# Second products split over two loops, and one more block of attention in row form

## The chip, the cores and the metric

The kernel runs on one core of one Trainium2 chip. The metric is the device time of one execution in microseconds; the median of three runs of the kernel before is 274.97 us (273.76 to 275.08). The profile is of one further execution, with its own time. Engines are named as in the profile: PE is TensorE (PEld its weight loads), DVE VectorE, ACT ScalarE, POOL GpSimd and SP SyncE; the last two mostly issue DMAs here.

## The reference: linear attention, then a two-layer network

Inputs are q, k, v of shape 8 x 8 x 576 x 64 (batch, head, position, width) and a norm weight g of 64; w_in is 512 x 2048, w_out 2048 x 512, alpha 2048, all in float32.

```
kv  = einsum('bhsd,bhse->bhde', k, v)
o   = einsum('bhsd,bhde->bhse', q, kv)
o   = o / sqrt(mean(o*o, axis=-1) + 1e-6) * g_norm
x   = o.transpose(0, 2, 1, 3).reshape(4608, 512)
h   = x @ w_in
g   = maximum(h, 0) + alpha * minimum(h, 0)
out = g @ w_out
```

There is no softmax. The network takes most of the arithmetic: two products of 4608 x 512 x 2048.

## The kernel before

The 4608 rows of x are cut into nine windows of 512 (W), numbered w = 0 to 8; the eight batches are called blocks b and have 576 rows, so a window covers the end of one block and the start of the next. Everything on TensorE is float16 with float32 sums in PSUM.

**First product.** For a window, a loop of 16 units u makes h in groups of 128 of the 2048 columns: four matmuls of 512 columns into one PSUM bank (`m1_mm`, L507). `m1_evac` then has ScalarE write max(-h, 0) (L514) and VectorE add it, weighted by 1 - alpha, to h; that gives `gt`, the activation in float16 (L518). From w=2 on, two banks, h1 and h2, take turns for h (three in w=1). For windows from W_ROW on, the first unit is "late": the first 384 columns (`m1_cols`, L530), some second products, then the last 128 columns.

**Second product.** Window 0 uses plain matmuls (`y_mm`, L539). Windows 1 to 8 use a Winograd form of Strassen's method on 2 x 2 blocks: seven products instead of eight, each of 16 matmuls of 256 columns (`prod_mm`, L688). Products 1 and 2 read `gt` and `w_out` alone. Products 6, 7, 5 and 3 read sums of `gt` blocks that VectorE makes (`s_sum`, s1 to s4, L623 to L629). Results collect in three sets called X (products 1, 2), Y (6, 7, 4) and Z (5, 3); `y_read` takes them out of PSUM: p1 and c11 on ScalarE, u2, u3, c21, c22 and c12 on VectorE. c11 to c22 are the output's quarters, which are then stored. In the kernel before, all seven products of window w-1 are made in the loop of window w, seven matmuls to each unit, and those of window 8 after the last loop. X and Z share one bank and Y has the other (`ps_y` and h0, swapped from window to window).

**Attention.** Attention of window w+1 is worked into the loop of w by tables from the unit to the step (`ATT_1`, `ROW_AT`, `QT_AT`). Windows 0 to 2 take the "column" form: q is transposed on TensorE (`step_t`, L327), k·v is made by head pairs (`step_kv`, L371) and masked on VectorE, q·kv comes out transposed (`step_ot`, L393), squares are made on ScalarE (L400) and summed by a matmul with a mask (`ssq_mm`, L416), and `norm` (L429) multiplies by 1/rms and g into xt. From W_ROW = 3 on comes the "row" form: q is transposed by DMAs on SP (`dma_t`, L361), `row_kv` (L1001) makes k·v by heads, `rows_mm` (L452) makes four tiles of 128 rows, `rows_sq` squares a tile on ScalarE (L463), `rows_ssq` sums it by head on VectorE (L469), `rows_rs` makes 1/rms on ScalarE (L479), and `rows_norm` multiplies on VectorE (L487) and issues a transposing DMA on SP into xt (L492). The row form leaves g out, so w_in is multiplied by g by ScalarE during the w=2 loop (`scale_w_in`, L246).

**Loads.** POOL issues loads (`load_gated` at the start of each loop) and most stores; SP issues transposes and the stores of c12. k is put in another order by ScalarE or VectorE (`regroup`, L195 and L197) before it is used.

**What sets the order.** It is written by hand: each engine runs its own instructions in program order, waits on semaphores where data or a buffer is not ready, and nothing overtakes. The loop `for w in range(1, NW)` at L1056 and the tables before it are that order.

Of the kernel before, what the change touches and what calls it, by code (L numbers as in the profile page):

```python
# [17 lines left out]
def kernel(  # L18
# [32 lines left out]
    W_ROW = 3  # L51
# [94 lines left out]
    for i in range(NBUF):  # L146
        t = {}
        for nm in ("k", "v", "q") if i < 2 else ("k", "v"):
            n = 1 if nm == "v" else T0 if i == 0 else NT
            t[nm] = qkv_p.tile([P, n, H, D], FP16, name=f"{nm}sb{i}")  # L150
            if i > 0 or nm == "v":
                nc.vector.memset(t[nm][REM:P, n - 1, :, :], 0.0)
        bufs.append(t)
    stages = {}

    def load0(nm, j, n=1):
        i, h = divmod(2 * j, HH)
        if (0, nm, i) not in stages:
            stages[0, nm, i] = stage_p.tile([P, HH, T0, D], FP16, name=f"{nm}st", tag=f"{nm}st")
# [5 lines left out]
    def load_main(b, nm, h0=0, h1=H):  # L165
        if (b, nm) not in stages:
            stages[b, nm] = stage_p.tile([P, H, TPP, D], FP16, name=f"{nm}st", tag=f"{nm}st")
# [5 lines left out]
    def load_q(b):  # L173
        st = stage_p.tile([P, TPP, H, D], FP16, name="qst", tag="qst")
# [7 lines left out]
    def buf_of(b, nm):  # L182
        return bufs[min(b, B_NAT) % 2 if nm == "q" else b % NBUF][nm]

    def load_rem(b, nm):
        nc.gpsimd.dma_start(
            out=buf_of(b, nm)[0:REM, 0 if nm == "v" else TPP, :, :],
# [16 lines left out]
    def load_gated(b):  # L204
        load_rem(b, "q")
        if b == B_NAT:
            load_q(b)
        load_rem(b, "k")
        load_main(b, "k")
        if b > B_NAT:  # L210
            load_q(b)
        load_rem(b, "v")
        load_main(b, "v")

# [6 lines left out]

    def regroup_pair(b, nm, j):
        regroup(b, nm, 2 * j, 2 * j + 2, nc.scalar)

# [17 lines left out]
    def scale_w_in(g):  # L242
        i = max(n for n, f0 in enumerate(IN_CUTS[:-1]) if f0 <= g * P)
        f0 = g * P - IN_CUTS[i]
        blk = w_in_sb[i][:, :, f0 : f0 + P]
        nc.scalar.activation(out=blk, in_=blk, func=AF.Copy, scale=g2col[:])  # L246
# [56 lines left out]
    kv_masked = [const_p.tile([P, NPAIR, P], FP16, name=f"kv_masked{i}") for i in range(2)]  # L303
# [52 lines left out]
    def dma_t(b, ts=tuple(range(NT))):  # L356
        qt = qt_sb[b % 2][:, :, PAD : PAD + S]
        for t in ts:
            c0, c1 = t * P, min((t + 1) * P, S)
            src = stages[b, "q"][:, t] if t < TPP else buf_of(b, "q")[0:REM, TPP]  # L360
# [6 lines left out]
    def step_kv(b, j, pool=(ps_s, "s")):  # L367
# [10 lines left out]
        kvs[b, j] = kv_masked[b % 2][:, j, :]  # L378
# [5 lines left out]
    def step_ot(w, j, pool=None, parts=1):  # L384
# [13 lines left out]
        sq = attn_p.tile([P, W], FP16, name="sq_sb")  # L398
# [27 lines left out]
    def norm(w, j, parts=1):  # L426
        ot_ps, rstd = ots.pop((w, j))
        for c in col_parts(parts):
            nc.vector.scalar_tensor_tensor(  # L429
# [9 lines left out]
    def rows_mm(w, i0):  # L439
        o_ps = row_tile([2, 2, NPAIR, D], "or_ps")  # L440
        for i in (i0 + 1, i0):
            b, r = divmod(w * W + i * P, S)
            for j in range(NPAIR):
# [5 lines left out]
                for n, (bb, c) in enumerate(steps):  # L449
                    for h in range(2):  # L450
                        part = slice(h * D, (h + 1) * D)
                        nc.tensor.matmul(  # L452
                            out=o_ps[:, h, i - i0, j, :],
# [4 lines left out]
            ots[w, "r", i] = o_ps[:, :, i - i0]  # L458

    def rows_sq(w, i):  # L460
        o_ps = ots.pop((w, "r", i))
        sq = attn_p.tile([P, 2, NPAIR, D], FP16, name="sq_sb")
        nc.scalar.activation(out=sq[:], in_=o_ps, func=AF.Square)  # L463
        ots[w, "r", i] = (o_ps, sq)

    def rows_ssq(w, i):
        o_ps, sq = ots.pop((w, "r", i))
        ssq = attn_p.tile([P, 2, NPAIR], FP32, name="ssq_r")
        nc.vector.tensor_reduce(  # L469
            out=ssq[:].rearrange("p h j -> p (h j)"),  # L470
            in_=sq[:].rearrange("p h j d -> p (h j) d"),
            axis=mybir.AxisListType.X, op=ALU.add,
        )
        ots[w, "r", i] = (o_ps, ssq)

    def rows_rs(w, i):
        o_ps, ssq = ots.pop((w, "r", i))
        rstd = attn_p.tile([P, 2, NPAIR], FP32, name="rstd_r")
# [33 lines left out]
    def m1_evac(h_ps, w, g):  # L512
        m_sb = gt_p.tile([P, W], FP32, name="m_sb", bufs=2)
        nc.scalar.activation(out=m_sb[:], in_=h_ps[:], func=AF.Relu, scale=-1.0)  # L514
        i, r = divmod(g, 2)
        if (w, i) not in gts:
            gts[w, i] = gt_p.tile([P, 2, W], FP16, name="gt", tag=f"gt{i}")
        nc.vector.scalar_tensor_tensor(  # L518
            out=gts[w, i][:, r, :], in0=m_sb[:], scalar=beta_sb[:, g : g + 1], in1=h_ps[:],
            op0=ALU.mult, op1=ALU.add,  # L520
        )

# [22 lines left out]
    store_turn = [0]  # L545

# [620 lines left out]
```

## Time and profile before

| what | value |
|---|---|
| median of 3 runs | 274.97 us (273.76 to 275.08) |
| the profiled execution | 275.59 us, span 273.6 us |
| granted TensorE clock in it | 0.994 |
| busy: PE, DVE, ACT | 266.3, 227.9, 155.9 us |
| first product L507 | 544 matmuls of 512 columns, 136.9 us by durations |
| VectorE's sum L518 | 144 of 744 ns |
| ScalarE's negated copy L514 | 144 of 599 ns |
| squares L463, reductions L469, of row tiles | 24 of 599 ns, 24 of 678 ns |

Durations of matmuls overlap (they are pipelined), so a rate on TensorE is read from the starts of successive rows. In a group of the profile, the first figures are busy time and mean duration; what stands behind the bar is the idle time before them, and who ended it. The chain of waits is followed back from the last instruction.

The loop of w=1 runs from about 48.1 to 66.8 us, w=2 to 94.5, w=3 to 122.1, w=4 to 149.8, and each of the next ones takes about as long; the products of window 8 run from 257.8 us on.

### The profile page before, as it was taken

The page shows a single profiled execution, that of the slowest core. Times are in us where ns is not written, and L with a number is a line of the kernel's source. Part 1 is how long each engine was busy: PE and PEld are TensorE (multiplying, and loading weights), DVE is VectorE, ACT ScalarE, POOL GpSimd, SP SyncE. Part 2 cuts the span into 40 slices and gives each one's busy share as a digit, 9 for nine tenths or more (in the row PEclk, how much of TensorE's full clock was granted, in tenths as well). Part 3 has the DMA queues.
Part 4 walks back from the last instruction along what each step waited for, and adds up shares of the span by engine and source line. Part 5 has one row for each costly group of instructions (what it writes and reads, how often), then busy time and mean ns, then how long its engine had stood idle before and what let it go on. Part 6 is the DMA issues. An engine that isn't in the chain of part 4 may idle for free.

```text
span 273.6 us, 5687 instructions
## 1 busy us (share of the span) xinstructions
PE 266.3 (97%) x2181; PEld 170.8 (62%) x2181; DVE 227.9 (83%) x432; ACT 155.9 (57%) x294; POOL 86.2 (32%) x123
## 2 busy tenths in 40 slices
PE   7799999999999999999999999999999999999995
PEld 2364464555666766666666666666666666666794
DVE  6459938899889979997999799979998999877863
ACT  3267555879989865645565556555544553443210
POOL 8773462780733355226421551100110012000200
PEclk9799999999999999999999999999999999999999
DMA  8999999999999689966996699720222122201223
GB/s 161 196 200 199 197 202 189 220 112 162 137 164 180 99 129 149 170 153 113 155 167 147 112 156 164 151 89 19 77 60 77 22 77 60 77 1 41 77 79 116
DMA packets 87343, 34.56 MB, mean 126 GB/s; under 512 B 58884, under 2 KB 85652, under 8 KB 87316
## 3 DMA queue, kind: packets, MB, share of 16 engines
q0 software_dynamic: 58064, 24.35, 69.5%
q1 hardware_dynamic: 28212, 8.83, 17.1%
q10 hardware_dynamic: 1040, 1.02, 1.2%
q8 instruction: 17, 0.28, 0.4%
q14 instruction: 10, 0.08, 0.1%
HBM read 36.71 MB, written 9.44 MB: 169 GB/s over the span
## 4 chain that ended last, share of the span: by engine, by line
PE 95%; DMA 2%; DVE 1%; issue 0%; ACT 0%; POOLq 0%
PE h_ps L507 43%; PE yY L688 15%; PE yX L688 10%; PE yZ L688 10%; PE y L539 5%; DMA vst<-in_v_dram 2%; PE h_ps L530 2%; PE kv_ps L371 2%; PE or_ps L452 1%; PE kv_ps L1001 1%; PE ssq_ps L416 1%; PE qt_ps L327 1%; PE ot_ps L393 1%; PE yZ L683 1%; PE warm_ps L295 0%
## 5 line engine op out<-in xcount | busy, mean ns | idle before, releaser
L507 PE MATMUL h_ps<-xt,w_in_sb 128*128 128x512 f16 x544 | 136.9, 379 | 0.0
L514 ACT ACTIVATE m_sb<-h_ps 128x512 f32<-128x512 f32 x144 | 86.1, 599 | 78.1 <-PE h_ps L507 67.7
L518 DVE SCALAR_TENSOR_TENSOR gt<-m_sb,beta_sb,h_ps 128x512 f16<-128x512 f32 x144 | 106.2, 744 | 24.1 <-ACT m_sb L514 22.5
L507 PEld LDWEIGHTS <-w_in_sb 128*128 128x128 f16 x544 | 52.1, 98 | 40.0
L550 POOL DMA_DIRECT2D out_dram<-y_sb x36 | 22.6, 630 | 134.3 <-ACT y_sb L726 53.4
L688 PEld LDWEIGHTS <-s 128*128 128x128 f16 x496 | 48.5, 98 | 19.1
L688 PEld LDWEIGHTS <-gt 128*128 128x128 f16 x384 | 37.3, 98 | 14.0
L688 PE MATMUL yY<-wsum,s 128*128 128x256 f16 x256 | 36.3, 273 | 0.0
L688 PE MATMUL yX<-w_out_sb,gt 128*128 128x256 f16 x256 | 36.1, 273 | 0.0
L177 POOL DMA_DIRECT2D qst<-in_q_dram x20 | 17.7, 923 | 1.8 <-DMA vst<-in_v_dram 1.8
L688 PE MATMUL yY<-wsum,gt 128*128 128x256 f16 x128 | 17.6, 273 | 0.0
L688 PE MATMUL yZ<-wsum,s 128*128 128x256 f16 x120 | 16.7, 273 | 0.0
L688 PE MATMUL yZ<-w_out_sb,s 128*128 128x256 f16 x120 | 16.7, 273 | 0.0
L487 DVE TENSOR_TENSOR x_rows<-or_ps,rstd_r 128x512 f16<-128x512 f32 x24 | 16.4, 683 | 0.0
L469 DVE TENSOR_REDUCE ssq_r<-sq_sb 128x8 f32<-128x512 f16 x24 | 16.3, 678 | 0.0
L463 ACT ACTIVATE sq_sb<-or_ps 128x512 f16<-128x512 f32 x24 | 14.4, 599 | 2.6 <-PE or_ps L452 2.6
L539 PE MATMUL y<-w_out_sb,gt 128*128 128x512 f16 x64 | 15.8, 379 | 0.0
L625 DVE TENSOR_TENSOR s<-s,gt 128x512 f16<-128x512 f16 x32 | 13.5, 421 | 0.5
L623 DVE TENSOR_TENSOR s<-gt 128x512 f16<-128x512 f16 x32 | 13.4, 418 | 0.0
L629 DVE TENSOR_TENSOR s<-gt,s 128x512 f16<-128x512 f16 x32 | 13.2, 417 | 0.0
L627 DVE TENSOR_TENSOR s<-gt 128x512 f16<-128x512 f16 x32 | 13.0, 418 | 0.0
L720 DVE TENSOR_TENSOR u<-yY,p 128x512 f32<-128x512 f32 x16 | 10.9, 683 | 1.9 <-PE yY L688 1.7
(88 smaller groups left out, 249.9 us busy)
## 6 DMA issues: line engine op xcount, KB each, us to landing
out_dram<-y_sb POOLq DMA_DIRECT2D x16, 256.0 KB, 2.7
kst<-in_k_dram POOLq DMA_DIRECT2D x7, 512.0 KB, 7.9
vst<-in_v_dram POOLq DMA_DIRECT2D x6, 512.0 KB, 10.5
qst<-in_q_dram POOLq DMA_DIRECT2D x20, 128.0 KB, 8.0
w_out_sb<-in_moe_w_out_dram POOLq DMA_DIRECT2D x8, 256.0 KB, 11.7
out_dram<-y_sb SPq DMA_DIRECT2D x5, 256.0 KB, 2.2
w_in_sb<-in_moe_w_in_dram POOLq DMA_DIRECT2D x2, 512.0 KB, 10.0
qst<-in_q_dram POOLq DMA_DIRECT2D x2, 512.0 KB, 12.1
```

Of the source, the lines that this page charges most:

```text
L177: nc.gpsimd.dma_start(out=st[:, t, :, :], in_=srcs["q"][b, :, t * P : (t + 1) * P, :].rearrange("h p d -> p h d"),)
L463: nc.scalar.activation(out=sq[:], in_=o_ps, func=AF.Square)
L469: nc.vector.tensor_reduce(out=ssq[:].rearrange("p h j -> p (h j)"), in_=sq[:].rearrange("p h j d -> p (h j) d"), axis=mybir.AxisListType.X ...
L487: nc.vector.tensor_tensor(out=xr[:].rearrange("p j h d -> p h j d"), in0=o_ps, in1=rstd[:].unsqueeze(3).to_broadcast([P, 2, NPAIR, D]), op ...
L507: nc.tensor.matmul(out=h_ps[:], lhsT=w_in_blk(c, g), rhs=xts[w][:, c, :], start=(c == 0), stop=(c == NC - 1),)
L514: nc.scalar.activation(out=m_sb[:], in_=h_ps[:], func=AF.Relu, scale=-1.0)
L518: nc.vector.scalar_tensor_tensor(out=gts[w, i][:, r, :], in0=m_sb[:], scalar=beta_sb[:, g : g + 1], in1=h_ps[:], op0=ALU.mult, op1=ALU.add,)
L539: nc.tensor.matmul(out=y[:], lhsT=gt_cols(w, g, a * P, (a + 1) * P), rhs=w_out_blk(g), start=(g == 0), stop=(g == NF - 1),)
L550: engs[store_turn[0] % len(engs)].dma_start(out=dst, in_=src)
L623: nc.vector.tensor_add(out=t[:], in0=a21, in1=a22)
L625: nc.vector.tensor_sub(out=t[:], in0=sums[w, 1, k][:], in1=a11)
L688: nc.tensor.matmul(out=bank, lhsT=lhs, rhs=rhs, start=fresh, stop=(c == NK - 1), skip_group_check=True,)
```

## The change

- Products 1 and 2 of window w now run in the loop of w itself (`x_prods`, tables X_1, X_AT, X_LAST), as groups of `gt` become ready; their last four run in the first two units of the next loop. The other five run in the next loop in the order 6, 7, 4, 5, 3 (`yz_prods`). X has the bank of `ps_y`, and Y and Z follow one another in h0. Units keep seven second products from w=3 on.
- In units 2, 5, 8, 11 and 14 of a loop from w=2 on, VectorE reads a finished product before it makes the unit's own sum (`m1_neg` and `m1_sum` instead of `m1_evac`).
- The s sums get new places (S_AT, S_1, S_2, S_LAST) and one buffer each.
- Window 2 is in row form (W_ROW = 2); block 2's q is transposed by DMAs from its regrouped copy.
- `rows_ssq` goes: ScalarE squares each head of a row tile by itself, with its sum over 64 columns as a second output, eight instructions to a tile.
- `row_kv` reads k as it was loaded, so that the regrouping copies of k for blocks 2 to 7 go; blocks 6 and 7 are made together. `kv_masked` holds four blocks.
- w_in is multiplied by g before and at the start of the w=1 loop, mostly on VectorE, and `norm` leaves g out for window 1.
- Loads are placed by a table (LOADS); those of block 3 and some others wait for a "gate", a copy of one element by POOL that needs a certain group of `gt`. Stages of k and v have three buffers. Three of window 0's four stores come later, on SP.
- The products after the last loop come in another order (LAST).

```diff
-    W_ROW = 3
+    W_ROW = 2
...
+    def rem_of(b, nm):
+        one = nm == "v" or nm == "k" and b % NBUF == 2
+        return buf_of(b, nm)[:, 0 if one else TPP, :, :]
...
+    def scale_w_in(i, h=0, n=1, eng=None):
+        f = (IN_CUTS[i + 1] - IN_CUTS[i]) // n
+        blk = w_in_sb[i][:, :, h * f : (h + 1) * f]
+        if eng is nc.scalar:
+            nc.scalar.activation(out=blk, in_=blk, func=AF.Copy, scale=g2col[:])
+        else:
+            nc.vector.tensor_scalar(
+                out=blk, in0=blk, scalar1=g2col[:], scalar2=None, op0=ALU.mult
+            )
...
     def rows_sq(w, i):
         o_ps = ots.pop((w, "r", i))
-        sq = attn_p.tile([P, 2, NPAIR, D], FP16, name="sq_sb")
-        nc.scalar.activation(out=sq[:], in_=o_ps, func=AF.Square)
-        ots[w, "r", i] = (o_ps, sq)
-
-    def rows_ssq(w, i):
...
-        nc.vector.tensor_reduce(
+        sq = attn_p.tile([P, 2, NPAIR, D], FP16, name="sq_sb", bufs=4)
+        ssq = attn_p.tile([P, 2, NPAIR], FP32, name="ssq_r", bufs=4)
+        for h in range(2):
+            for j in range(NPAIR):
+                nc.scalar.activation(
+                    out=sq[:, h, j], in_=o_ps[:, h, j], func=AF.Square,
+                    accum_out=ssq[:, h, j : j + 1],
+                )
...
-    Y_ORDER = (1, 6, 2, 7, 5, 4, 3)
-    Y_LIST = [(n, i) for n in Y_ORDER for i in range(2 * NK)]
-    PER = len(Y_LIST) // NF
...
+    X_LIST, YZ_LIST = products(1, 2), products(6, 7, 4, 5, 3)
+    X_AT = [0, 0, 1, 2, 2, 1, 2, 2, 1, 2, 2, 1, 2, 2, 1, 7, 2, 2]
+    X_1 = [0] * 9 + [4, 4, 4, 4, 0, 5, 7, 2, 2]
+    X_LAST = [0, 0] + [1] * 8 + [2] * 4 + [0] * 4
+    YZ_AT = [5, 5, 6] * 5 + [0]
+    YZ_1 = [0, 8, 8] + YZ_AT[3:]
+    YZ_READS = {2: "u2", 5: "u3", 8: "c21", 11: "c22", 14: "c12"}
...
+    for i in range(4):
+        scale_w_in(i)
...
+    for h in range(4):
+        scale_w_in(4, h, 4, nc.scalar)
...
+    def row_kv(bs):
...
+                            lhsT=head_rows(b, "k", 2 * j + i, t),
+                            rhs=head_rows(b, "v", 2 * j + i, t),
...
     ROW_AT = {
+        2: dict(
+            mm={1: ((0,),), 7: ((1, 2), (3,))}, kv={6: (2,)}, sq=(1, 7, 8, 9),
+            rs=(4, 9, 10, 11), norm=(4, 9, 10, 11),
         ),
+        3: dict(
+            kv={3: (3,)}, mm={4: ((1, 0), (3, 2))}, sq=(4, 5, 6, 8), rs=(6, 7, 9, 12), norm=(6, 7, 9, 12),
+        ),
+        4: dict(
+            kv={0: (4,)}, mm={1: ((1, 0), (3, 2))}, sq=(1, 3, 5, 8), rs=(4, 6, 9, 12), norm=(4, 6, 9, 12),
+        ),
...
+    QT_AT = {
+        2: {1: ((2, 0), (2, 1), (2, 2)), 14: ((3, 0), (3, 1), (3, 2)), 15: ((2, 3), (2, 4))},
+    }
...
+    def gate(src):
+        nc.gpsimd.tensor_copy(out=gate_sb[:], in_=src)
+
+    LOADS = {
+        (1, 1): (("gate", 0), ("q", 3)),
+        (1, 7): (("gate", 6), ("k", 3)),
+        (1, 14): (("gate", 13), ("v", 3)),
+        (2, 1): (("q", 4), ("k", 4), ("v", 4)),
+        (2, 2): (("put", 0), ("put", 2), ("put", 1)),
...
         for u in range(NF):
             late = w >= W_ROW and u == 0
+            behind = w > 1 and u in YZ_READS
+            h_ps = h_bank()
             if late:
-                h_ps = h_bank()
-                m1_cols(h_ps, w, G_ORDER[u], 0, W - P)
+                m1_cols(h_ps, w, u, 0, W - P)
             else:
-                m1_group(w, G_ORDER[u])
...
+                m1_mm(h_ps, w, u, range(NC))
+                m1_neg(h_ps, w, u)
+                if not behind:
+                    m1_sum(h_ps, w, u)
+            unit_sums(w, u)
+            if u < 2 and w > 1:
+                x_prods(w - 1, NF + u)
+            x_prods(w, u)
             if w > 1:
-                unit_sums(w, u)
...
+                yz_prods(w - 1, u)
+            if behind:
+                m1_sum(h_ps, w, u)
+            if late:
+                m1_cols(h_ps, w, u, W - P, W)
+                m1_evac(h_ps, w, u)
+                unit_sums(w, NF)
+            if w == 1 and u < 4:
+                scale_w_in(5, u, 4)
```

## The prediction

> **What bounds the kernel now.** I read the page's chain of work first, then TensorE's own waits, then the timelines of TensorE, ScalarE and VectorE around the change, then a table of the loops.
>
> ```profile
> span 273.6 us, 5687 instructions
> ...
> PE 266.3 (97%) x2181; PEld 170.8 (62%) x2181; DVE 227.9 (83%) x432; ACT 155.9 (57%) x294; POOL 86.2 (32%) x123
> ...
> PE 95%; DMA 2%; DVE 1%; issue 0%; ACT 0%; POOLq 0%
> ```
> The chain is TensorE from end to end. Its own waits are few, and the longest are in the first 16 us:
> ```profile
> PE warm_ps L295 <- DVE y_sb L119: 1.5, 1, 1.5
> PE kv_ps L371 <- DMA vst<-in_v_dram: 1.2, 1, 1.2
> PE qt_ps L327 <- DVE qsb L763: 0.4, 1, 0.4
> PE kv_ps L371 <- DVE ksb L217: 0.3, 1, 0.3
> PE ot_ps L393 <- DVE kv_masked L379: 0.2, 1, 0.2
> ```
> The timeline (start us, us) gives the pace inside a loop, and the pieces of block 2 that the change replaces:
> ```profile
> 131.87 1.03 PE L507 MATMUL h_ps<-xt,w_in_sb 128*128 128x512 f16 x4
> 132.73 0.93 PE L688 MATMUL yX<-w_out_sb,gt 128*128 128x256 f16 x7
> 133.49 1.03 PE L507 MATMUL h_ps<-xt,w_in_sb 128*128 128x512 f16 x4
> ...
> 48.95 0.44 PE L327 MATMUL qt_ps<-ident,qsb 128*128 128x128 f16 x5
> 49.23 1.89 PE L507 MATMUL h_ps<-xt,w_in_sb 128*128 128x512 f16 x8
> ...
> 98.70 0.64 PE L452 MATMUL or_ps<-kv_masked,qt_sb 64*128 64x64 f16 x32
> 99.27 1.04 PE L507 MATMUL h_ps<-xt,w_in_sb 128*128 128x512 f16 x4
> ```
> Starts, not durations, count: four first products take 0.86 us (0.216 each), seven second products 0.76 (0.109 each), so a unit is 1.63 us and the next begins at once. From 16 us to 270 us TensorE has no hole that a filling could use. Only less TensorE work makes the kernel faster, and every new wait makes it slower. The ScalarE rows on which the rest hangs:
> ```profile
> 132.93 0.60 ACT L514 ACTIVATE m_sb<-h_ps 128x512 f32<-128x512 f32 x1 [0.97 <-PE h_ps L507]
> 133.42 0.59 ACT L463 ACTIVATE sq_sb<-or_ps 128x512 f16<-128x512 f32 x1
> ...
> 143.19 0.29 ACT L479 ACTIVATE rstd_r<-ssq_r,eps_t 128x8 f32<-128x8 f32 x1
> 143.38 0.60 ACT L195 COPY ksb<-kst 128x512 f16<-128x512 f16 x1
> ```
> A 512-column activation holds ScalarE for 0.49 (132.93 to 133.42), the 8-column one for 0.19. In the units of the w=4 loop the negated copy starts 1.06 after the unit, VectorE's sum 0.66 after that (133.59) for 0.745: a bank of h is free again about 1.45 us after its copy starts, 2.5 after its unit starts. With two banks it is wanted at 3.26, so the copy may be 0.75 late.
>
> **The change part by part**, against the profiled execution (275.59 us; span 273.6; 0.62 above the median of 274.97, which I take off at the end).
>
> *Block 2 in row form.* Gone from TensorE, by starts between 48.9 and 64.8: transposes 0.28+0.28+0.27+0.27, K·V 0.55+0.56, q·KV 0.44+0.22+0.26, sums of squares 4 x 0.22: 4.0 us. Added: 40 small K·V products as at 71.73 to 72.49 (0.76) and 32 row products (98.70 to 99.27, 0.57), in three pieces, 0.1 for seams: 1.4. Net -2.6, all on the chain. Here a page speaks against the gain: Perfetto Trace Analysis (the Trainium skill), Identifying the Most-Contended Engine, calls matmul busy time a bad measure and weight-load time a good one. By its measure (62%) there is headroom and -2.6 might be worth 0. The start-to-start rows show none, so I keep -2.6.
>
> *Two of seven products in the block's own loop.* 28 of 0.109 (3.05 us) move from the w=2 loop into w=1, the tail goes from 112 to 96; the sum over all is the same. Cost 0 while units hold seven. They fill w=1 only from unit 9; earlier units are 0.865 long, where VectorE needs 0.665 for the sum and 0.33 to 0.6 for a scaling of w_in in units 0 to 3; three banks absorb this.
>
> *Five products in one bank.* The reads u2, u3, c21, c22, c12 now come before the unit's own sum. Products end at 1.63, visible 0.16 later, read 0.61, sum 0.745: bank free at 3.17 against 3.26. Slack 0.09; the next product on that bank is due at 2.6, the read done at 2.5. Cost 0, bounds 0 and 0.1 in each of 35 units (3.5). VectorE can hold it because 24 reductions (L469, 0.61 each by starts) leave it. The next loop's opening in w=2 puts eight s sums (0.34 each) around the late sum; unit 1's sum is then about 0.2 late: +0.2.
>
> *Squares with an accumulator.* One 0.49 us square per row tile becomes eight of 64 columns, each with a one-column sum, 28 tiles, 224 instructions. No row shows that form. Two squares at 39.56 take 1.09 together, 0.495 apart; a 256-column one lasts 0.382 against 0.595 for 512 (L400), 0.83 ns a column; so 64 columns hold ScalarE 0.115. For the sum written out: nothing (0.115); the price of a one-column operand, as L420's rows start 0.57 apart against 0.49 for L400, +0.08 (0.195); an instruction of its own at the spacing of the smallest row, +0.19 (0.305). A tile then costs X = 0.92, 1.56 or 2.44. I take the first: the 64-column square is the same function on the same tile, and both surcharges are from instructions with an extra input, not output. The others are kept as ends. ScalarE: Activation LUTs (the Trainium skill), What ACT_TABLE_LOAD costs, gives 186 ns plus 0.833 a column less 93 of overlap: an estimate of 0.146 and X = 1.17, which would change the sum by 0.1; it says nothing of a written sum, and no run here shows one.
> What X does: after the copy, the tile keeps ScalarE until 1.56+X, and the next copy wants it at 2.69. In loops 3 to 7 a wait on TensorE appears when X passes 1.13+0.75, about 1.95 with the tile's own start. In w=2 (tiles in units 4, 5, 6) and w=1 (units 7, 8, 9, only 0.87 to 1.3 long) backlogs add up. Stepping copy, squares, sum and bank through these units: X=0.92 costs 0; 1.56 costs 2.0 in w=1 and 0.65 in w=2; 2.44 costs 5.6, 3.5 and 20 tiles x 0.49 = 9.8.
>
> *Queues.* SP gets five q transposes for block 2 and four x_rows transposes, 1.2 us of issue each; SP issues nothing between 2.3 and 63.6 us now. The first three can start after the q regroup (48.2), the last lands 3.3 to 6.9 (row of qt_sb) after 50.7, 54.0 to 57.6; TensorE wants it at 56.6: 0 taken, bounds 0 and 1. The three early stores move to SP behind block 3's transposes; the fourth stays on POOL. POOL is held by a gate on the loop's first gt, with q3 behind it; by one on g 6 with k3; by one on g 13 with v3. With my unit lengths (loop from 48.1, unit 13 at 63.1) g 13 is ready at 65.5, V's DMA is issued at 66.5 and, by its row, lands 6.7 to 11.7 later. Row K·V of block 3 wants it at 73.5. I take 74.0, near the short end because no k or q load is ahead of it: +0.5, bounds 0 and 4.7. Later loads have a loop to spare.
>
> *Off the chain.* 18 k copies (0.61) and 16 scalings (0.72) leave ScalarE; four 1024-column scalings enter VectorE at 33.5, where it is idle from 36.6 to 38.8: 0 at 0.33 each (the spacing of such copies), 1 us on TensorE if each takes 1.2. The last row tile is normalized one unit later (12), but seven products stand before its columns are read: ready about 7 us after unit 12, wanted at 7.9: 0, if its 2.3 to 4.4 us transpose is not held.
>
> Sum: -2.6 + 0.2 + 0.5 = -1.9: 273.7 for such an execution, **273.1** beside the median.
>
> **The rivals.**
> *A: the sum costs a little (X about 1.56).* For: the only one-column operand that the trace prices costs 0.08. Against: it is an input. Place: units 7 to 13 of w=1, where the first products wait for h banks. -1.9 + 2.65 = +0.75: 275.7, no change.
> *B: ScalarE becomes the bound, slower.* One mechanism: each written sum is an instruction of its own. For: the 8-column row holds ScalarE 0.19 however small. Against: ScalarE is busy only 16 of 27.7 us in the w=4 loop, so on average there is room. It decides from X = 1.7 on (about 277); at 2.44 it is -1.9 + 18.9, 292. Between, with 0.24 an instruction (X 1.9), about 278.
> *C: the loads come late.* v3 at 11.7 us and q's transposes last: -1.9 + 4.2 + 1 = +3.3, 278. For: loads in these loops landed in 9.4 to 10.3. Against: those shared the rings with k and q.
> *D: the change wins nothing, because w=1 turns from TensorE-bound to VectorE-bound.* VectorE there is busy 16.4 of 18.7 us; after it 16 x 0.665 + 4 x 0.34 + 4 x 0.4 + 4 x 0.61 = 16.0 of 18.9. That covers little; if all of -2.6 were lost: 275.0.
>
> **How the numbers follow.** Less than about 0.5% can't be told from no change in this kernel (273.6 to 276.3). Forecast 0.42, its own range 272.3 (all of -2.6) to 273.6. A with D 0.21. B 0.28, half of it below 281. C 0.09, a third of it inside the 0.5%. Faster 0.42, same 0.23, slower 0.35. The range runs from 272.2 to 281; what is left out is the dear half of B and little below.
>
> **What would show it.** Right: no transposes by TensorE between 48 and 60 us; TensorE without waits in w=1; squares of 64 columns starting 0.12 to 0.13 apart; unit starts 1.63 apart from w=3 on; K·V of block 3 waiting for vst under 1 us. Wrong: rows between the squares or starts 0.2 and more apart; first products waiting for gt in units 4, 6, 9; h waits in units 10 to 13 of w=1; a wait of several us for vst near 73.

## The result, and the profile after

The changed kernel takes **290.34 us** (median, 288.94 to 291.40); the kernel before, run beside it, 275.02 (273.76 to 275.37). The ratio is 1.0568, 95% interval 1.0520 to 1.0616: slower by 15.3 us, where 1.9 us of gain was forecast. That is above the forecast range (272.2 to 281.0). An execution more than 1.5% above the fastest of the same kernel is left out of the medians and ratios below (one of four in e1 and e10, two of four in e4).

The page of the changed kernel: span, busy time, chain.

```profile
span 289.3 us, 6117 instructions
...
PE 270.0 (93%) x2205; PEld 169.4 (59%) x2205; DVE 216.3 (75%) x410; ACT 165.6 (57%) x680; POOL 85.3 (29%) x123
...
PE 62%; DMA 18%; ACT 10%; DVE 5%; issue 3%; SPq 1%; DVEq 0%; POOLq 0%
```

The chain was TensorE for 95%; now DMAs have 18% of it and ScalarE 10%. VectorE lost 11.6 us of work and ScalarE gained 9.7, yet neither is near full. So it is no engine that became the bound on average; single waits did. TensorE's own waits (total, times, longest):

```profile
PE h_ps L538 <- DMA xt<-x_rows: 5.6, 3, 2.4
PE h_ps L507 <- DVE gt L522: 2.5, 5, 1.0
PE yY L700 <- DVE s L639: 1.8, 5, 0.4
PE warm_ps L293 <- DVE y_sb L119: 1.5, 1, 1.5
PE kv_ps L1037 <- DMA vst<-in_v_dram: 1.2, 1, 1.2
PE or_ps L456 <- DMA qt_sb<-qsb: 1.1, 1, 1.1
```

Before, the list held nothing after the first 16 us. The largest is new: the first product of a loop (L538, the opening of the loop) waits for the transposed row tiles. Its places in TensorE's timeline (start us, us, and the wait):

```profile
100.24 0.93 PE L700 MATMUL yX<-w_out_sb,gt 128*128 128x256 f16 x7
103.57 0.81 PE L538 MATMUL h_ps<-xt,w_in_sb 128*128 128x384 f16 x4 [2.40 <-DMA xt<-x_rows]
...
132.40 0.93 PE L700 MATMUL yX<-w_out_sb,gt 128*128 128x256 f16 x7
135.67 1.46 PE L538 MATMUL h_ps<-xt,w_in_sb 128*128 128x384 f16 x4 [2.33 <-DMA xt<-x_rows]
```

Seven products take 0.76, so the hole is 103.57 - 100.24 - 0.76 = 2.57, and 2.5 at the second. It costs more than itself. The windows around the first hole (columns: stretch, length, busy time and instructions of PE, PEld, DVE, ACT and POOL, granted clock, DMA share, GB/s):

```profile
100.00:104.00 4.00, 1.60 (x12) 1.00 (x11) 2.45 (x5) 0.60 (x1) 0.00 (x0) 1.00 1.19 186
104.00:108.00 4.00, 4.00 (x57) 2.76 (x55) 1.46 (x3) 1.33 (x3) 0.00 (x0) 0.60 0.30 75
```

In the first stretch TensorE is busy for 1.60 of 4 us; in the next it is busy throughout, at a clock of 0.60.

Loop by loop, from the starts of the first products (us; "early loads" and "mended" are versions of the next section):

| loop | before | changed | early loads | mended |
|---|---|---|---|---|
| w=2 | 27.7 | 34.35 | 30.54 | 28.63 |
| w=3 | 27.58 | 32.10 | 28.57 | 27.62 |
| w=4 | 27.71 | 29.81 | 28.23 | 27.70 |
| w=5 | 27.58 | 28.77 | 28.78 | 28.26 |
| w=6 | 27.71 | 28.35 | 28.08 | 26.84 |
| w=7 | 26.73 | 27.26 | 27.26 | 26.73 |
| w=8 to the end | 41.8 | 39.5 | 39.5 | 39.3 |

Most of the loss lies in w=2 and w=3 (5.7 and 4.5 against the mended version), where loads and transposes meet.

### The profile page after: what moved, and what is told of

The parts are those of the page before. It is cut to its first block, busy times and chain, and to the rows that moved or that the text cites. A ratio compares the mean times of both kernels' runs of the same rounds, so it can differ in the third digit from the quotient of the medians.

```text
span 289.3 us, 6117 instructions
## 1 busy us (share of the span) xinstructions
PE 270.0 (93%) x2205; PEld 169.4 (59%) x2205; DVE 216.3 (75%) x410; ACT 165.6 (57%) x680; POOL 85.3 (29%) x123
## 4 chain that ended last, share of the span: by engine, by line
PE 62%; DMA 18%; ACT 10%; DVE 5%; issue 3%; SPq 1%; DVEq 0%; POOLq 0%
PE h_ps L507 26%; PE yY L700 11%; DMA xt<-x_rows 8%; PE yZ L700 7%; ACT sq_sb L470 6%; PE yX L700 6%; DMA qst<-in_q_dram 5%; ACT m_sb L516 4%; PE y L547 3%; DMA qt_sb<-qsb 3%; DMA vst<-in_v_dram 2%; PE h_ps L538 2%; SPq L362 1%; PE kv_ps L1037 1%; DVE gt L522 1%
## 5 line engine op out<-in xcount | busy, mean ns | idle before, releaser
L516 ACT ACTIVATE m_sb<-h_ps 128x512 f32<-128x512 f32 x144 | 88.0, 614 | 88.5 <-PE h_ps L507 62.9
L559 POOL DMA_DIRECT2D out_dram<-y_sb x32 | 20.5, 643 | 143.1 <-ACT y_sb L738 60.5
L470 ACT ACTIVATE sq_sb<-or_ps 128x64 f16<-128x64 f32 x224 | 47.0, 270 | 1.9 <-PE or_ps L456 1.8
L700 PE MATMUL yX<-w_out_sb,gt 128*128 128x256 f16 x256 | 47.5, 274 | 0.0
L470 ACT ACTIVATION_READ_ACCUMULATOR sq_sb<-or_ps 128x1 f32 x224 | 46.5, 256 | 0.0
L700 PE MATMUL yY<-wsum,s 128*128 128x256 f16 x256 | 37.1, 277 | 1.8 <-DVE s L639 1.8
L487 DVE TENSOR_TENSOR x_rows<-or_ps,rstd_r 128x512 f16<-128x512 f32 x28 | 19.1, 683 | 2.2 <-ACT rstd_r L479 2.2
L700 PE MATMUL yZ<-wsum,s 128*128 128x256 f16 x120 | 17.5, 273 | 0.0
L538 PE MATMUL h_ps<-xt,w_in_sb 128*128 128x384 f16 (+1 forms) x56 | 9.5, 299 | 5.6 <-DMA xt<-x_rows 5.6
L635 DVE TENSOR_TENSOR s<-gt 128x512 f16<-128x512 f16 x32 | 13.4, 418 | 0.0
## 6 DMA issues: line engine op xcount, KB each, us to landing
vst<-in_v_dram POOLq DMA_DIRECT2D x6, 512.0 KB, 11.6
w_out_sb<-in_moe_w_out_dram POOLq DMA_DIRECT2D x8, 256.0 KB, 11.6
```

What stands on the lines that cost most here:

```text
L470: nc.scalar.activation(out=sq[:, h, j], in_=o_ps[:, h, j], func=AF.Square, accum_out=ssq[:, h, j : j + 1],)
L487: nc.vector.tensor_tensor(out=xr[:].rearrange("p j h d -> p h j d"), in0=o_ps, in1=rstd[:].unsqueeze(3).to_broadcast([P, 2, NPAIR, D]), op ...
L516: nc.scalar.activation(out=neg[w, g][:], in_=h_ps[:], func=AF.Relu, scale=-1.0)
L538: nc.tensor.matmul(out=h_ps[:, c0:c1], lhsT=w_in_blk(c, g), rhs=xts[w][:, c, c0:c1], start=(c == 0), stop=(c == NC - 1), skip_group_check= ...
L559: engs[store_turn[0] % len(engs)].dma_start(out=dst, in_=src)
L635: nc.vector.tensor_add(out=t[:], in0=a21, in1=a22)
```

## The experiments

| label | what it is | median us | ratio to before, 95% interval |
|---|---|---|---|
| e1_one_square | one square a tile | 283.43 | 1.0329 (1.0277 to 1.0381) |
| e2_loads | loads a unit earlier | 282.75 | 1.0302 (1.0266 to 1.0338) |
| e3_both | both | 280.22 | 1.0170 (1.0103 to 1.0237) |
| e4_reduce | squares as before | 283.85 | 1.0341 (1.0265 to 1.0417) |
| e5_v_s | e2, V early, s3 sum early | 284.90 | 1.0371 (1.0345 to 1.0398) |
| e6_all | e5 with squares as before | 282.40 | 1.0273 (1.0256 to 1.0289) |
| e7_before_acc | kernel before, accumulating squares | 280.01 | 1.0181 (1.0163 to 1.0200) |
| e8_norm10 | changed, last tile earlier | 290.32 | 1.0566 (1.0520 to 1.0613) |
| e9_gate | e6 with the gate back | 278.83 | 1.0162 (1.0123 to 1.0201) |
| e10_sp_order | e8, q transposes behind | 289.75 | 1.0577 (1.0512 to 1.0642) |
| e11_scale | e9, scalings on ScalarE | 279.46 | 1.0172 (1.0136 to 1.0207) |
| e12_kv4 | "mended": e9, V late, K·V later | 275.17 | 1.0032 (1.0013 to 1.0051) |
| e13_w1 | e12, VectorE relieved | 274.67 | 1.0013 (0.9999 to 1.0028) |
| e14_acc | e12 with accumulating squares | 279.43 | 1.0202 (1.0166 to 1.0239) |

The kernel before had medians of 274.43 to 274.74 beside them. The ratios are of means.

### Squares or loads

Theory 1 was that the squares alone cost the 15 us, theory 2 that late loads do a good part. One square of 512 columns with one written sum in place of eight pieces (e1 and e3 leave out the mean by head: 1/rms is taken over all heads at once):

```diff
-        for h in range(2):
-            for j in range(NPAIR):
-                nc.scalar.activation(
-                    out=sq[:, h, j], in_=o_ps[:, h, j], func=AF.Square,
-                    accum_out=ssq[:, h, j : j + 1],
-                )
+        nc.scalar.activation(
+            out=sq[:], in_=o_ps, func=AF.Square, accum_out=ssq[:, 0, 0:1],
+        )
```

> Edit: a row tile is squared by one activation of 512 columns with one written sum over all of them (one read of the accumulator), instead of eight of 64 columns with eight reads; 1/rms is then taken over all heads at once, so the mean by head is left out. Nothing else moves. In the changed kernel a tile keeps ScalarE 1.57 us (121.71 to 123.28); here about 0.6. Theory 1, ScalarE's squares are the whole cause (they hold the h banks and make the row tiles late, and so their transposes): the 17.9 us over the dense time of 272.4 go, 272 to 275. Theory 2, two causes, ScalarE's squares and late loads: only the waits for h banks and sums go (2.4 in w=1, 1.6 in w=2, five times 0.4 for the last s3 sum), the waits of TensorE for transposed row tiles at the starts of w=3 and w=4 stay: 283 to 286.

Measured: 283.43, 6.9 us gained. The waits for gt in w=1 and for s in each loop go; the openings of loops get no better (three waits for x_rows, 4.2 in all, and one more of 3.1).

The loads earlier, and all of block 2's q transposes together:

```diff
-        2: {1: ((2, 0), (2, 1), (2, 2)), 14: ((3, 0), (3, 1), (3, 2)), 15: ((2, 3), (2, 4))},
+        2: {1: tuple((2, t) for t in range(5)), 14: ((3, 0), (3, 1), (3, 2))},
...
-        (2, 1): (("q", 4), ("k", 4), ("v", 4)),
+        (2, 0): (("q", 4), ("k", 4), ("v", 4)),
...
-        (3, 1): (("q", 5), ("k", 5), ("v", 5)), (3, 14): (("gate", 13), ("k", 6), ("v", 6)),
-        (4, 1): (("q", 6), ("k", 7), ("v", 7)), (5, 1): (("q", 7),),
+        (3, 0): (("q", 5), ("k", 5), ("v", 5)), (3, 14): (("gate", 13), ("k", 6), ("v", 6)),
+        (4, 0): (("q", 6), ("k", 7), ("v", 7)), (5, 0): (("q", 7),),
```

> Edit: all five transposes of block 2's q are issued in unit 1 of w=1 (two were issued behind block 3's in units 14 and 15), and the loads of LOADS at unit 1 of w=2 to 5 stand at unit 0, ahead of c11's store on POOL. Squares as in the changed kernel. Theory 1 (squares alone): no more than 2 us gained, 288 to 290. Theory 2 (late loads crowd out the transposes of the row tiles): the wait for q's transposes in w=2 (1.25), the waits at the starts of w=3, w=4 and w=6 (2.6, 2.5, 0.8) and the slow clock after them (1.9 and 1.7) go for the most part: 279 to 283.

Measured: 282.75, 7.6 us gained with the squares untouched. Of 5.6 us of waits for x_rows at the openings 0.5 is left. The loads and the q transposes were not moved apart from each other.

Why a unit in a table is worth so much is read from POOL's timeline. In the changed kernel:

```profile
81.72 0.71 POOL L195 DMA_DIRECT2D qsb<-in_q_dram  x1 [6.85 <-DMA qt_sb<-qsb]
...
88.14 0.96 POOL L173 DMA_DIRECT2D vst<-in_v_dram  x1
...
109.98 1.66 POOL L559 DMA_DIRECT2D out_dram<-y_sb  x3 [13.10 <-ACT y_sb L738]
111.64 0.72 POOL L195 DMA_DIRECT2D qsb<-in_q_dram  x1
```

and in the kernel before:

```profile
70.20 0.69 POOL L186 DMA_DIRECT2D qsb<-in_q_dram  x1 [9.81 <-DMA qt_sb<-qsb]
...
76.57 0.97 POOL L168 DMA_DIRECT2D vst<-in_v_dram  x1
...
99.23 0.70 POOL L186 DMA_DIRECT2D qsb<-in_q_dram  x1 [3.15 <-DMA qt_sb<-qsb]
```

Block 4's loads wait for a buffer that the last q transpose of block 2 reads. That transpose stands in unit 15 now, so the loads go out 12.5 us into the w=2 loop (81.72 - 69.22) instead of 3.4 (70.20 - 66.8). Block 5's stand behind the store of c11 on POOL and go out 8.1 us into the w=3 loop (111.64 - 103.57) instead of 4.8 (99.23 - 94.48). They then run beside the four transposes of the row tiles, which the chain shows (start us, us, what):

```profile
73.65 7.50 DMA qt_sb<-qsb
...
94.21 9.22 DMA xt<-x_rows
...
127.60 8.02 DMA xt<-x_rows
```

Such a transpose lands 2.4 us after its issue where no load is beside it, and 8 to 9 here. DMA: Bandwidth & Descriptors (the Trainium skill), Issuing engines are not separate DMA queues, says that DMAs started by ScalarE, SyncE or GpSimd run on the same 16 DMA engines and interleave; the 2.4 and 9.2 us fit that.

Both edits together:

> Edit: the one square with one sum of the first run (mean by head left out) and the early loads of the second together. Theory 1: as the first run, 272 to 275. Theory 2: both gains add, 273 to 276, with 1.4 us left for block 3's V.

Measured: 280.22, not 273 to 276. The gains overlap, and new waits take their place: V of block 3 (2.2 us), a q transpose (1.3).

Squares and reductions as in the kernel before:

```diff
+        nc.scalar.activation(out=sq[:], in_=o_ps, func=AF.Square)
...
+        nc.vector.tensor_reduce(
+            out=ssq[:].rearrange("p h j -> p (h j)"),
+            in_=sq[:].rearrange("p h j d -> p (h j) d"),
+            axis=mybir.AxisListType.X, op=ALU.add,
+        )
```

> Edit: the squares as in the kernel before (one activation of 512 columns, sums by head by a reduction on VectorE, 0.61 us each by starts, one or two units after), all else as changed. The output is the full one. Theory 1: 272 to 276. Theory 2: as the first run, or up to 3 us more where VectorE has no room: 283 to 289.

Measured: 283.85, a gain of 6.5; the openings still wait 5.4 us for x_rows. Theory 1 falls: with whole squares 283.4 and 283.9 us remain. Theory 2 holds.

### One wait at a time

```diff
-        (1, 7): (("gate", 6), ("k", 3)),
-        (1, 14): (("gate", 13), ("v", 3)),
+        (1, 7): (("gate", 6), ("k", 3), ("v", 3)),
...
-        3: ((-1, 3, 2),), 4: ((-1, 3, 3),), 6: ((-1, 4, 1),), 9: ((-1, 4, 2),),
+        3: ((-1, 3, 2), (-1, 3, 3)), 6: ((-1, 4, 1),), 9: ((-1, 4, 2),),
```

> The changed kernel with its loads one unit earlier, all q transposes of block 2 in unit 1 of the first block's loop, block 3's V loaded right behind its K in unit 7 (instead of unit 14), and the sum -1,3,3 in unit 3 instead of 4. The squares stay in accumulating pieces. The kernel with the early loads alone took 282.75, with 1.25 us of wait for vst and five waits of 0.5 for s left. Theory of many causes (each of these waits is its own): both go, 282.75 - 1.25 - 2.5 = 279.0 (278.0 to 280.0), and the 2.5 us of h waits in the w=1 loop stay. Rival (the squares alone hold VectorE and ScalarE, so that moved work only waits elsewhere): no gain, 282 to 283.

Measured: 284.90, 2.2 us worse than e2. The two waits that it aimed at went, as expected: no wait for s, none for vst in w=2. A larger one came: w=2 opened 3.7 us late. e6 adds the reductions of e4.

> The same with the squares as in the kernel before, one 512-column square and VectorE's reduction, in the units after the square. Theory of many causes: the h waits of the w=1 loop (2.5) and of w=2 (1.4) go too, 279.0 - 3.9 = 275.1; the reductions give VectorE 0.61 each again, so some s sums may be late by up to 0.5 a loop: 274 to 277. If so nothing of the 2.6 us that TensorE saves is left after all waits, or up to 1 us. Rival (VectorE can't hold five reads ahead of the sums and the reductions too): 279 or more, with waits for s and gt in every loop.

Measured: 282.40, with the same late opening (3.0). Its cause was my own edit. The wait for g 13 went with V's old place, so POOL went straight on to block 4's loads; in POOL's timeline of e6:

```profile
59.95 0.92 POOL L173 DMA_DIRECT2D vst<-in_v_dram  x1
60.83 0.72 POOL L195 DMA_DIRECT2D qsb<-in_q_dram  x1
61.50 3.56 POOL L182 DMA_DIRECT2D qst<-in_q_dram  x4
```

and the row tiles' transposes of that time (first and last start; landing):

```profile
L496 SPq DMA_TRANSPOSE xt<-x_rows x4: 1189/1231/1342, 55.8 to 65.9; - x4
...
DMA to landing us min/median/max: 6.8/7.0/7.3
```

In the changed kernel itself these four land after 2.4 in the median. The data that the gate waits for are not what the load needs; what it does is keep these transfers apart. e9 gives it back:

```diff
+        (1, 14): (("gate", 13),),
```

> The version with VectorE's reductions, early V and early s3 sum (282.4), with one line given back: GpSimd waits for g 13 again before it issues block 4's loads. In the two versions without that wait GpSimd went straight on, block 4's q, k and v were issued from 60.8 us instead of 70.0, and the four row tiles' transposes of block 2 landed 6.8 to 7.3 us after issue (2.4 with the wait); w=2 opened 3.0 and 3.7 us late, with a clock of 0.64 behind it. Theory (those loads beside these transposes are what opened w=2 late): that wait goes, with 1.8 us of slow clock; V of block 3 arrives without a wait: 282.4 - 3.1 - 1.8 = 277.5 (276 to 278.5). Rival (V of block 3 itself, now beside the transposes, holds them): w=2 still opens 2 us or more late, 280.5 to 282.5.

Measured: 278.83, against 282.40 without it; the opening of w=2 is 1.5 us late instead of 3.0 (the profile now puts it down to a sum s of VectorE, which that product does not read). Both theories have a part: the loads of block 4 half of the wait, V beside the transposes probably the rest.

### The squares alone

The kernel before with nothing but the accumulating squares:

```diff
-        nc.scalar.activation(out=sq[:], in_=o_ps, func=AF.Square)
...
+                nc.scalar.activation(
+                    out=sq[:, h, j], in_=o_ps[:, h, j], func=AF.Square,
+                    accum_out=ssq[:, h, j : j + 1],
+                )
```

> The kernel before with one part of the change alone: the squares of its row tiles (24 tiles, blocks 3 to 8) in eight accumulating pieces each, and no reduction by VectorE. A tile then holds ScalarE about 1.57 instead of 0.49 us. By the threshold of the prediction (a wait appears when a tile passes about 1.9 us) it costs nothing in the loops from w=3 on; it frees VectorE of 0.61 a tile. Theory that the price of the squares is paid only where the units are short (w=1, w=2): 274.5 to 276, within 0.5% of the kernel before. Rival (ScalarE's queue delays copies, sums and norms everywhere): 24 tiles by 0.3 to 0.5, 282 to 287.

Measured: 280.01, 5.3 us slower; I had expected nothing. The w=2 loop is 3.0 us longer, each later one 0.3. ScalarE's groups in the changed kernel show why a piece costs more than a square of 64 columns:

```profile
L470 ACT ACTIVATE sq_sb<-or_ps 128x64 f16<-128x64 f32 x224 | 47.0, 270 | 1.9 <-PE or_ps L456 1.8
L470 ACT ACTIVATION_READ_ACCUMULATOR sq_sb<-or_ps 128x1 f32 x224 | 46.5, 256 | 0.0
```

and its timeline how long:

```profile
121.71 0.22 ACT L470 ACTIVATE sq_sb<-or_ps 128x64 f16<-128x64 f32 x1
121.81 0.20 ACT L470 ACTIVATION_READ_ACCUMULATOR sq_sb<-or_ps 128x1 f32 x1
121.90 0.23 ACT L470 ACTIVATE sq_sb<-or_ps 128x64 f16<-128x64 f32 x1
...
123.28 0.66 ACT L516 ACTIVATE m_sb<-h_ps 128x512 f32<-128x512 f32 x1
```

The written sum is an instruction of its own, 0.10 from the square's start to its own and 0.10 to the next square: 0.197 a piece, (123.28 - 121.71) = 1.57 a tile. In this version ScalarE keeps the k copies of 0.6 us and, in w=2, the 16 scalings of w_in of 0.72 us; in w=2 it is busy without a gap (4.00 of 4 us from 78 and from 86 us). There it is the bound.

### Which tile the openings wait for

```diff
-rs=(4, 6, 9, 12), norm=(4, 6, 9, 12),
+rs=(4, 6, 9, 10), norm=(4, 6, 9, 10),
```

> The changed kernel, loads and squares as they are, with the last row tile of each block normalized, and so transposed, in unit 10 instead of unit 12, 3.3 us earlier. In the changed kernel that transpose landed 8.0 and 9.2 us after it was issued and the loops w=3 and w=4 opened 2.4 and 2.3 us late, with a slow clock behind it. Theory that the last tile's transpose is what these loops wait for: the opening waits go (4.7 us) and the slow clock with them (1.9 and 1.65): 290.3 - 8 = 282 (281 to 285). Rival (the queues are full whatever the order, so an earlier issue lands no earlier): 288 to 291 with waits of 2 us left at the openings.

Measured: 290.32, no gain. The edit moved a tile that the openings do not wait for. The first product of a loop reads 384 columns, the first three row tiles; the last tile's 128 columns are read by the second piece (`m1_cols` runs twice). In the changed kernel that piece runs without a wait:

```profile
138.41 0.63 PE L538 MATMUL h_ps<-xt,w_in_sb 128*128 128x128 f16 x4
```

SP's timeline of the changed kernel has the third tile's transpose, the fourth q transpose and the last tile's transpose:

```profile
127.60 1.91 SPq L492 DMA_TRANSPOSE xt<-x_rows  x1
129.60 1.70 SPq L362 DMA_TRANSPOSE qt_sb<-qst  x1
131.40 1.24 SPq L492 DMA_TRANSPOSE xt<-x_rows  x1
```

The chain above has the first of them, issued at 127.60 and landed at 135.62, just ahead of the opening at 135.67. So the 9.2 and 8.0 us, which the expectation gives to the last tile, are the third tile's. That tile is normalized in unit 9, and e8 leaves it there: VectorE made its rows from 123.69 to 124.38, but SP came to their transpose only at 127.75. SP's timeline of e8:

```profile
115.78 4.51 SPq L492 DMA_TRANSPOSE xt<-x_rows  x2
120.38 7.28 SPq L362 DMA_TRANSPOSE qt_sb<-qst  x3
127.75 3.23 SPq L492 DMA_TRANSPOSE xt<-x_rows  x2
```

Three q transposes of the next block stand ahead in SP's order and hold it for 7.28 us, 2.4 each, where one takes 1.2 in the quiet parts. (The profile shows SP no wait for q's load there, as my expectation of the next run has it; they are slow to issue.) So e10 puts them behind:

```diff
-            QT_AT[w] = {7: first + rest[0:1], 10: rest[1:2], 13: rest[2:]}
+            QT_AT[w] = {10: first + rest[0:2], 13: rest[2:]}
```

> The changed kernel with the last row tile normalized in unit 10, and the next block's q transposes in unit 10 behind that tile's transpose instead of in unit 7 ahead of it. With the tile in unit 10 alone nothing was won (290.3): its rows were ready at 125.3 us, but SP issued their transpose at 129.8, after 7.3 us on three q transposes that stood ahead of it. Theory (SP's order: the tiles' transposes stand behind q transposes that wait for late loads and are slow to issue): the openings of w=4 and w=5 lose their waits of 1.7 and 2.3 us and the slow clock behind them, 1.65 each; that of w=3, where the transpose itself takes 9 us, stays; the q transposes land later, and the row products may wait up to 1 us in each loop: 290.3 - 7.3 + 1.5 = 284.5 (283 to 287). Rival (the rings are full, and the transposes land late in any order): 289 to 292, with 2 us left at each opening.

Measured: 289.75, no gain. The openings of w=4 and w=5 lost their waits, as the theory had it, since the third tile's transpose now stands ahead of the q transposes too (issued at 124.63, landed at 132.10); the loop before w=4 fell from 31.8 to 28.4 us. The wait at w=3 stayed. But the q transposes then landed too late for the row products of w=4:

```profile
PE or_ps L456 <- DMA qt_sb<-qst: 4.4, 1, 4.4
PE h_ps L538 <- DMA xt<-x_rows: 2.6, 1, 2.6
```

The sum stays. In these two runs the order on SP only chooses who waits; the time of the loads is the cause, since e2, which moves nothing but loads and block 2's q transposes, takes these waits away.

### What is left, and whether the saving exists

```diff
-                scale_w_in(5, u, 4)
+                scale_w_in(5, u, 4, nc.scalar)
```

> The version of the first run of this set with the four scalings of w_in in units 0 to 3 of w=1 on ScalarE instead of VectorE. That loop still has two waits for h banks there (0.56 at 54.0, 0.83 at 65.3 us), and VectorE is busy without a gap from 47.9 to 55.7. Theory (w=1 is bound by VectorE, the prediction's rival D): the first wait goes, and 1.6 to 2.4 us less on VectorE also softens the second: 0.6 to 1.5 us faster than that run. Rival (the chain of copy, sum and bank bounds it, in which ScalarE stands too): no change, or up to 1 us slower, since ScalarE's copies then stand behind the scalings.

Measured: 279.46 against 278.83, intervals overlapping: no gain. The wait of 0.56 became 0.43; the other stayed, since ScalarE stands in the same chain.

```diff
-        (1, 7): (("gate", 6), ("k", 3), ("v", 3)),
-        (1, 14): (("gate", 13),),
+        (1, 7): (("gate", 6), ("k", 3)),
+        (1, 14): (("gate", 13), ("v", 3)),
...
-kv={3: (3,)}, mm={4: ((1, 0), (3, 2))}, sq=(4, 5, 6, 8), ssq=(5, 6, 7, 10), rs=(6, 7, 9, 12), norm=(6, 7, 9, 12),
+kv={4: (3,)}, mm={5: ((1, 0), (3, 2))}, sq=(5, 6, 7, 8), ssq=(6, 7, 8, 10), rs=(7, 8, 9, 11), norm=(7, 8, 9, 11),
```

> The best version so far (278.8) with block 3's V loaded in unit 14 of w=1 again, behind the four row tiles' transposes of block 2, and block 3's K.V and row products one unit later in w=2 (units 4 and 5), so that V has 1.6 us more; its last tile is normalized in unit 11. Theory (each transfer needs its own place; V beside the transposes opened w=2 1.5 us late): that wait goes and vst is waited for by less than 0.3: 278.8 - 1.5 = 277.3 (276.3 to 278.3). It stays slower than the kernel before (274.5), since the h waits of w=1 (1.9), the opening of w=3 (0.7) and its q transposes (1.1) have no place yet. Rival (the wait moves again): 278.5 to 280.5, with a wait for vst, qt_sb or xt of 1 us or more in w=2 or at the opening of w=3.

Measured: 275.17, 3.7 us gained where 1.5 was expected: V, the opening of w=3 and the q transposes all come in time. (V's place, the later K·V and the last tile's earlier unit were not told apart.) All that the profile lists of TensorE's waits in it from 50 us on:

```profile
PE h_ps L511 <- DVE gt L526: 1.4, 2, 0.8
```

From the starts of its rows, TensorE's holes are 0.73, 0.20 and 0.98 in w=1, 0.41 and 0.24 in w=2: 2.56 together. Without them the span would be 273.8 - 2.56 = 271.2, against 273.6 of the kernel before, which has no such holes. So the change saves TensorE about 2.4 us (by the medians 1.9: 275.17 - 2.56 against 274.55), and that version loses them again to VectorE in w=1 and w=2. This is worked out from the holes; no version ran without them.

```diff
+        if (w, i) == (2, 3):
+            ssq = attn_p.tile([P, 2, NPAIR], FP32, name="ssq_r", bufs=4)
+            for h in range(2):
+                for j in range(NPAIR):
+                    nc.scalar.activation(
+                        out=sq[:, h, j], in_=o_ps[:, h, j], func=AF.Square,
+                        accum_out=ssq[:, h, j : j + 1],
+                    )
...
-                scale_w_in(5, u, 4)
+                scale_w_in(5, u, 4, nc.scalar if u > 1 else None)
...
-16: ((-1, 1, 2), (-1, 2, 2), (-1, 1, 3), (-1, 2, 3)), 2:
+16: ((-1, 1, 2), (-1, 1, 3)), 1: ((-1, 2, 2), (-1, 2, 3)), 2:
```

> The mended version (275.17, waits left on TensorE: 0.73 at 54.4 and 0.98 at 65.7 in the w=1 loop, 0.41 at 74.1 in the opening of w=2) with three small relocations of VectorE's work: the third and fourth scaling of w_in in w=1 to ScalarE, the squares of block 2's last tile in accumulating pieces on ScalarE (one tile only, no reduction for it), two of the four s sums at the opening of w=2 one unit later. Theory (what is left is VectorE's load in these places, and TensorE's saving of 2.6 is real): -0.4, -0.5 and -0.3: 274.0 (273.3 to 274.6), at or just under the kernel before. Rival (ScalarE stands in the same chain, so the waits only change their name): 275 to 276.

Measured: 274.67 beside 274.55, ratio 1.0013: no difference from the kernel before. The holes of w=1 shrink from 1.9 to 1.0 us; the one at the opening of w=2 grows from 0.41 to 0.69, for the two sums are needed there. The profiled execution, 276.09, was the slowest of twelve; it holds one more wait of 1.2 at the opening of w=5, for which the profile names VectorE's s and no DMA. That product reads xt and w_in and no s, and two of the row tiles' transposes ahead of it landed 8.5 and 11.0 us after issue, so a late transpose is likelier; the third tile's own landing isn't in the profile. No version beat the kernel before.

Last, the accumulating squares put back into the mended version, nothing else:

> The mended version (275.17) with the accumulating squares of the change put back on every tile, nothing else: what the squares cost alone, once the loads are in time. The prediction's own working for a tile of 1.56 us gave 2.0 in w=1 and 0.65 in w=2 and nothing in later loops, from which 275.17 - 1.7 (the h waits of the reductions that go) + 2.5 + 0.8 = 276.8. Theory of a local price: 276.5 to 278, h waits of 2.5 in w=1 and 0.8 in w=2, none later. Rival (the squares hold the norms back, so the row tiles' transposes are late too): 279 or more, with waits for xt at loop openings.

Measured: 279.43, 4.3 us more (278.17 to 281.38). In its profiled execution, the fastest, the span is 2.6 us longer (276.4 against 273.8): TensorE waits 1.8 for gt, 0.5 once for x_rows, and 1.1 for a read of y on VectorE, which the chain follows back through a norm to ScalarE's squares. What the slower executions lose beyond that isn't shown. The price is not only local, as the rival had it, but the openings wait little.

## Why the prediction was wrong, point by point

- **"Later loads have a loop to spare"** is the step that failed, and the largest. They had none: issued 9 and 3 us later in their loops, by a buffer and by POOL's order, they ran beside the row tiles' transposes. Moving them, with block 2's q transposes, gave 7.6 us. I priced each load against its own reader, and never against the transfers that it runs beside, nor POOL's queue ahead of it. The profile before had shown the price: two row tiles' transposes issued while block 5's loads were under way landed after 7.7 and 7.8 us.

```profile
L492 SPq DMA_TRANSPOSE xt<-x_rows x2: 1190/1397/1604, 104.3 to 109.2; - x2
...
DMA to landing us min/median/max: 7.7/7.8/7.8
```

- **"The last row tile ... 0, if its 2.3 to 4.4 us transpose is not held."** The last tile's transpose took 5.6 us (131.40 to 137.03) and no wait came of it, so the 0 holds for that tile. What the openings waited for is the third tile, which the prediction doesn't price: its transpose landed 9.2 and 8.0 us after issue. e8 moves the last tile alone and wins nothing; e10 puts the third ahead of the q transposes, and the wait moves.
- **Squares, a = 0.115 and X = 0.92**: the second step that failed, mis-sized. Measured 0.197 and 1.57. (The prediction's own rows, 0.495 less 448 columns at 0.83 ns, give 0.12 and not 0.115.) Rival B had the mechanism (an instruction of its own), rival A the price (0.195, X 1.56). The skill's estimate of 0.146 was nearer than my choice, and short too. My table then gave 2.65 us for X = 1.56; the runs gave 4.3 in the mended version, 6.5 and 6.9 beside late loads (e4, e1), 2.5 where other waits took the place (e3, e6).
- **V of block 3, +0.5**: g 13 was ready at 68.2 instead of 65.5, and V landed 8.1 us after issue: 1.35.
- **q of block 2, 0**: right for the three early transposes. The last two of five, in unit 15, I hadn't placed at all: 1.25 us, and block 4's loads behind them.
- **Reads before the unit's own sum, 0 with bounds to 3.5**: no wait at an h bank came of them from w=3 on. There is one of 0.5 in each of five loops, 2.5 together, at s3's last sum. One unit earlier it is gone (e5); but it is gone in e1 and e4 too, where that sum stands where it did and only the squares are whole. So it is a price of the squares in the later loops, which the prediction put at 0. (The prediction's terms add up to 3.145 and not 3.17, and in the profile before ScalarE's copies start 0.20 and not 0.16 after the last product; with that the slack is 0.08.)
- **s sums at the opening of w=2, +0.2**: 0.41.
- **Block 2 in row form, -2.6**: right in the main; 1.9 to 2.4 is what the mended version's holes leave. The new pieces on TensorE are 0.75 for K·V, 0.22 and 0.46 for the rows, 1.43 where 1.4 was taken. Perfetto Trace Analysis, Identifying the Most-Contended Engine, would have called it headroom by weight loads alone, which were 62% of the span, and yet the saving is there beside the holes. The same section asks for MFU (matmul work against peak) with it, which the prediction left out.
- **Rivals.** C (late loads) had the right kind of cause and the wrong transfers: v3 and q cost 2.6 together, of 4.7 + 1 allowed, and the later loads far more. D is partly so: with the reductions back, w=1 has 1.9 us of holes (e12), and 1.0 where VectorE is relieved (e13); in the changed kernel the waits for gt there went with the squares (e1). B decides in stretches only: in the changed kernel ScalarE is busy 4.00 of 4 us from 60 and from 86 us, beside waits for gt, but over no whole loop. In the kernel before with the same squares it decides in w=2 (e7).

## What to carry to other kernels

Price a moved load against the transfers that it will run beside and the queue that it stands in, and not only against its own reader; a gate may be there to keep the DMA engines free and not for data. Look up which piece of a buffer a waiting product reads, before moving one. When a wait goes and the time stays, look for the same time elsewhere before doubting the edit: here V, q, row tiles and the opening of the loops exchanged one lateness. A second output isn't free until a row shows it.

## What the hardware showed that I hadn't expected

Both holes of 2.5 us on TensorE in the changed kernel are followed by a slow clock (for the first, see the two windows of the first section). A group of eight K·V pieces lasts longer just behind the opening of w=3 than behind that of w=4, where the clock is back by then:

```profile
105.69 0.42 PE L1037 MATMUL kv_ps<-vst,kst 128*64 128x64 f16 x8
...
138.98 0.32 PE L1037 MATMUL kv_ps<-vst,kst 128*64 128x64 f16 x8
```

TensorE: Matmul & The Clock Gate (the Trainium skill), What's actually happening, gives an idle window of about 3.4 us for the drop to half; here a hole of 2.5 us brought 0.60 on average over the next 4 us. From the opening of w=3 to the unit at 111.48 7.9 us pass, in the mended version 6.4: the hole cost 1.5 us more than itself. Not every such hole did it: behind those of 2.5 us in e8 (opening of w=5), 2.7 in e10 (w=3) and 3.3 in e1 (w=3) the clock is 1.00, and holes of up to 1.9 never did. Second, SP's transposes not only land later beside loads (5.6 to 10.6 us against 2.4): SP itself needs up to 2.8 us to issue one (e8), against 1.2.
